# Planner of a three-layer kernel: engine start times, eight warm-up products, and newly chosen order numbers

## Chip, cores and metric

One core of one Trainium2 chip runs the whole program in one launch. The metric is the device time of one execution in microseconds (us). Lower is better.

## The reference

Three layers follow each other on 4 x 576 tokens of width 512, in float32:

```python
q_d, k_d, v_d = means over 4 neighbouring positions       # 144 positions
out = repeat(softmax(q_d k_d^T / 8) v_d, 4) + softmax(mask(|i-j| < 4, q k^T / 8)) v
x = out, heads side by side                                # [4, 576, 512]
xk, xr = mu * x + (1 - mu) * x_prev
x1 = sigmoid(xr @ w_r) * (relu(xk @ w_k) ** 2 @ w_v)       # 512 -> 1024 -> 512
y  = x1 + relu(layer_norm(x1) * g @ w_ch1) @ w_ch2         # 512 -> 2048 -> 512
```

All weights arrive as 64-bit floats and are turned into 32-bit ones on the chip.

## The kernel before

**Work and stages.** The attention runs 16 times, once for each pair of heads of each of the four batches (`attention(n, ...)`, n = 0 to 15). TensorE transposes q and k for some n (`tq`; the others are transposed by VectorE, line 542), and makes the scores of the two heads inside a window (`sc`, line 629, each opened by a mask product on line 623), the scores of the means (`ds`), the transposed weights (`tp`), sums of v (`vs`, the first four n only), and the two outputs (`up`, `pv`). The result lands in `xT`, which holds one batch.

The first dense layer runs over six chunks of 384 tokens. Each takes `prep` (lines 796 to 806: `tmu`, then a high and a low part, `xrh`/`xrl` and `xkh`/`xkl`, for each of four slices of the width), `moe_r` (product `psr`, 36 matmuls of 512 columns), `moe_k` (product `psk`, 96 of 384), `accumulate` (product `psv`, 72 of 512), and `moe_x` (line 861, `r`). A product of float32 accuracy is three matmuls of high and low parts (`mm3`, lines 778 to 780). Chunk 0 needs attentions 0 to 3, chunk 1 needs 0 to 7, and so on, so attentions 4 to 15 lie among the products of chunks 0 to 2. The second dense layer runs three times over 768 tokens (products `psh` and `pso`).

**Weights.** `load_f32` (line 383 on) brings 128 rows of a weight in with one transfer of 512 KB (line 389), into one of two buffers (`w`); ScalarE (lines 395, 397) and VectorE (402, 406) make the 32-bit number of it. `load_split` then makes a high part (line 375 on ScalarE or 376 on VectorE) and a low part (line 420). `wr0l` is the low part of rows 0 to 127 of w_r, `wk31l` that of slice 3, half 1 of w_k.

**What sets the order.** Nothing is issued while the kernel is written down: `add` (line 77) notes each operation with its engine, an estimated cost and a priority. `Plan.order` (line 122) then plays the operations through with these costs, an engine at a time: of what is ready, the one that can start first goes next, with ties decided by priority. It gives each engine its order, and where an operation may run on several engines (`either`, `copy`, `psum_copy`), its engine. The priorities are sums of the numbers in `PRM` (line 24). One of them, `thin`, is a limit in us: when TensorE has done short attention products for longer than it, these rank behind the dense ones. All transfers are issued by SyncE, in the planned order.

`Plan.issue` (line 228) walks through that order. Until the bank of the first `psv` is taken, it fills gaps that the plan shows on TensorE with warm-up products, whose result nobody reads (line 433):

```python
            if eng == "PE":
                if until.t is None:
                    for _ in range(int((o.at - free) / fill_cost)):
                        fill()
                free = o.at + cost
```

The planned gap divided by 0.14 us is the number of fillers. Besides these, 17 warm-up products are issued first of all (`warm_up`, line 431), and two ahead of each score of the first four attentions.

## Time and profile before

| | us |
|---|---|
| median of 3 runs | 773.99 |
| lowest and highest | 770.59, 775.18 |
| the profiled execution | 771.95 |
| its span, first to last instruction | 770.2 |
| TensorE busy in the span | 753.6 |
| VectorE, ScalarE, GpSimd busy | 524.6, 398.2, 63.8 |

The profile is of one execution. PE is TensorE's matmuls, PEld its weight loads, DVE is VectorE, ACT ScalarE, POOL GpSimd, and SP SyncE, whose queue (SPq) issues the transfers. Busy time is a share of the span; a matmul that waits inside its row is drawn busy. An arrow `[1.02 <-ACT ups]` behind a row is the engine's idle time before it and what ended it.

### The profile page before, as it was taken

The numbers are of one execution on the slowest core, as the hardware profiler recorded it, in microseconds if no ns is written. First come the engines' busy times: TensorE is split into PE (matmuls) and PEld (weight loads), VectorE is DVE, ScalarE is ACT, GpSimd is POOL, SyncE is SP. The second block draws the span as 40 slices with busy tenths as digits, with TensorE's granted clock in tenths as the row PEclk, the third lists the DMA queues.
The fourth block names the chain that finished last, engine by engine and source line by source line (L and its number), as shares of the span: only waits on it lengthen the run. The fifth ranks groups of instructions, "written<-read, shape, count | busy, mean of one in ns | idle before, by whom it ended". The sixth has DMA issues, their size and how long they took to land.

```text
span 770.2 us, 15665 instructions
## 1 busy us (share of the span) xinstructions
PE 753.6 (98%) x5816; PEld 650.2 (84%) x5816; DVE 524.6 (68%) x1083; ACT 398.2 (52%) x916; POOL 63.8 (8%) x113
## 2 busy tenths in 40 slices
PE   9999999999999999999999999999999999999997
PEld 6878787788788798888888888889889899889886
DVE  6899999998985959878889763486543364333233
ACT  6889997987884847868835431221421131111110
POOL 3101122112100000000110000020000020000000
PEclk9999999999999999999999999999999999999999
DMA  8997596867768895964689894379853347443322
GB/s 190 208 192 180 180 180 124 182 170 144 207 159 267 251 323 171 290 217 135 141 281 289 208 258 121 112 246 305 183 150 115 112 121 258 138 120 113 123 69 82
DMA packets 202854, 140.88 MB, mean 183 GB/s; under 512 B 127120, under 2 KB 160028, under 8 KB 202780
## 3 DMA queue, kind: packets, MB, share of 16 engines
q1 hardware_dynamic: 202780, 139.90, 66.6%
q8 instruction: 46, 0.75, 0.4%
q14 instruction: 28, 0.23, 0.1%
HBM read 107.88 MB, written 31.98 MB: 182 GB/s over the span
## 4 chain that ended last, share of the span: by engine, by line
PE 77%; DVE 10%; DMA 6%; ACT 4%; issue 2%; POOL 0%; SPq 0%; DVEq 0%; POOLq 0%; ACTq 0%
PE pso L779 8%; PE pso L778 8%; PE pso L780 8%; PE psh L778 7%; PE psh L779 7%; PE psh L780 7%; PE psk L778 4%; PE psv L778 4%; PE psk L780 3%; PE psk L779 3%; PE psv L779 3%; PE psv L780 3%; DMA w<-in_moe_w_ch_dram 3%; PE warm L433 2%; DVE tmu L802 1%
## 5 line engine op out<-in xcount | busy, mean ns | idle before, releaser
L778 PE MATMUL psh<-xn,sa 128*128 128x384 f32 x336 | 114.0, 339 | 2.4 <-DVE c L1114 1.2
L779 PE MATMUL psh<-xn,sa 128*128 128x384 f32 x336 | 113.6, 338 | 0.0
L780 PE MATMUL psh<-xn,sa 128*128 128x384 f32 x336 | 113.3, 337 | 0.0
L778 PEld LDWEIGHTS psh<-xn,sa 128*128 128x128 f32 x336 | 63.1, 188 | 11.0 <-DVE c L1114 2.1
L779 PEld LDWEIGHTS psh<-xn,sa 128*128 128x128 f32 x336 | 63.1, 188 | 6.1 <-DVE xn L1051 0.2
L780 PEld LDWEIGHTS psh<-xn,sa 128*128 128x128 f32 x336 | 63.1, 188 | 0.0
L379 ACT ACTIVATE c22h<-t 128x384 fp32r<-128x384 f32 x24 | 12.6, 525 | 83.7 <-DVE t L1106 78.6
L395 ACT ACTIVATE wf<-w 128x512 f32<-128x512 f32 x48 | 32.3, 673 | 17.4 <-DMA w<-in_moe_w_ch_dram 9.2
L402 DVE SCALAR_TENSOR_TENSOR wf<-wf,w 128x512 uint32<-128x512 uint32 x48 | 32.9, 687 | 11.1 <-ACT w L397 10.6
L379 ACT ACTIVATE kr<-psk 128x384 f32<-128x384 f32 x46 | 22.4, 488 | 25.2 <-PE psk L780 21.2
L379 ACT ACTIVATE c11h<-psh 128x384 fp32r<-128x384 f32 x23 | 11.3, 491 | 45.8 <-PE psh L780 45.7
L397 ACT ACTIVATE w<-w 128x512 uint32<-128x512 uint8 x52 | 35.0, 672 | 0.0
L843 DVE TENSOR_TENSOR kl<-kr,kh 128x384 fp32r<-128x384 f32 x43 | 23.8, 553 | 14.6 <-ACT kr L842 14.3
L1083 DVE SCALAR_TENSOR_TENSOR c11l<-psh,c11h 128x384 fp32r<-128x384 f32 x24 | 13.3, 554 | 29.1 <-ACT c11h L379 29.1
L802 DVE SCALAR_TENSOR_TENSOR tmu<-xT,oms,tmu 128x384 f32<-128x384 f32 (+1 forms) x64 | 31.7, 512 | 1.8 <-ACT tmu L796 1.8
L406 DVE SCALAR_TENSOR_TENSOR wf<-w,wf 128x512 uint32<-128x512 uint32 x48 | 32.7, 680 | 0.3
L1106 DVE TENSOR_TENSOR t<-psh,t 128x384 f32<-128x384 f32 x24 | 13.3, 554 | 28.5 <-PE psh L780 28.4
L1097 DVE TENSOR_TENSOR u<-psh,u 128x384 f32<-128x384 f32 x24 | 13.3, 555 | 27.2 <-PE psh L780 27.1
L379 ACT ACTIVATE c12h<-c 128x384 fp32r<-128x384 f32 x24 | 12.6, 525 | 37.0 <-DVE c L1110 36.9
L379 ACT ACTIVATE c21h<-c 128x384 fp32r<-128x384 f32 x24 | 12.6, 523 | 34.6 <-DVE c L1114 34.6
L796 ACT ACTIVATE tmu<-xT,vecs 128x384 f32<-128x384 f32 (+1 forms) x51 | 26.8, 539 | 6.9 <-DVE xrl L806 4.0
L1103 DVE TENSOR_TENSOR t<-psh,u 128x384 f32<-128x384 f32 x24 | 13.2, 552 | 20.2 <-PE psh L780 20.1
(527 smaller groups left out, 2164.5 us busy)
## 6 DMA issues: line engine op xcount, KB each, us to landing
sa<-s_dram SPq DMA_DIRECT2D x168, 256.0 KB, 2.7
w<-in_moe_w_ch_dram SPq DMA_DIRECT2D x32, 512.0 KB, 6.2
s_dram<-s SPq DMA_DIRECT2D x56, 256.0 KB, 4.0
vw<-in_v_dram SPq DMA_DIRECT2D x62, 96.0 KB, 4.0
x_dram<-r SPq DMA_DIRECT2D x18, 256.0 KB, 3.4
x1t<-x_dram SPq DMA_DIRECT2D x6, 768.0 KB
z_dram<-x1t SPq DMA_DIRECT2D x18, 256.0 KB, 2.7
zb<-z_dram SPq DMA_DIRECT2D x96, 48.0 KB, 2.8
```

The source lines that it names most:

```text
L379: return [("ACT", c_act(n, True), lambda: nc.scalar.activation(dst(), src(), AF.Relu), False), ("DVE", c_dve(n), lambda: nc.vector.tensor_ ...
L395: add("ACT", c_act(512), prio, lambda: nc.scalar.activation(f(), w64().bitcast(F32)[:, :, 1], AF.Abs, scale=2.0 ** -112), r=[w64], w=[f])
L397: add("ACT", c_act(512), prio, lambda: nc.scalar.activation(w64()[:, :, 0], w64().bitcast(U8).rearrange("p a (b c) -> p a b c", c=4)[:, :, ...
L402: lambda: nc.vector.scalar_tensor_tensor(fu(), fu(), 3, w64()[:, :, 0], op0=ALU.logical_shift_left, op1=ALU.bitwise_or),
L406: lambda: nc.vector.scalar_tensor_tensor(fu(), w64()[:, :, 1], 0x80000000, fu(), op0=ALU.bitwise_and, op1=ALU.bitwise_or),
L433: nc.tensor.matmul(warm()[:, :304], identb, isumb, start=True, stop=True)
L778: nc.tensor.matmul(ps, lh, rh, start=start, stop=False, skip_group_check=more)
L779: nc.tensor.matmul(ps, lh, rl, start=False, stop=False, skip_group_check=more)
L780: nc.tensor.matmul(ps, ll, rh, start=False, stop=stop, skip_group_check=more)
L796: add([("ACT", c_act(n, ap=1), lambda t=t, o=o, n=n, cur=cur, kt=kt: nc.scalar.mul(t()[:, o:o + n], cur(), mu[:, kt:kt + 1]), False), ("DV ...
L802: lambda t=t, o=o, n=n, prv=prv, kt=kt: nc.vector.scalar_tensor_tensor(t()[:, o:o + n], prv(), om[:, kt:kt + 1], t()[:, o:o + n], op0=ALU. ...
L843: add(either(C, lambda e: e.tensor_tensor(kl(), kr(), kh().bitcast(F32), op=ALU.subtract)), 0, prio, None, r=[kr, kh], w=[kl])
```

## The change

The planner lets each engine begin at a time of its own instead of at 0, and starts its count of fillers there; the first warm-ups are 8 instead of 17, with a planned cost of 1.55 us instead of 4.5; the loads of q and k of attention 0 are planned with a latency of 1.4 instead of 2.2 us; one small VectorE operation is planned with 0.35 instead of 0.18 us. All numbers of `PRM` that set priorities are new ones, chosen with a judge outside the kernel that halves TensorE's clock behind sparse stretches. Lines behind the second insertion stand five lower in the changed kernel (861 becomes 866), those before it two (389 becomes 391).

```diff
 PRM = dict(
-    thin=89.915, t0=-16.294, t1=-9.875, t2=6.158, t3=7.667, t4=48.796, t5=19.99, t6=6.382, t7=-23.592, t8=-0.47,
+    thin=2.825, t0=-27.784, t1=-16.919, t2=11.055, t3=15.08, t4=55.388, t5=22.947, t6=11.802, t7=-10.22, t8=4.811,
...
+    START = {"PE": 1.78, "ACT": 2.0, "DVE": 2.6, "POOL": 6.6, "SP": 0.74, "CTL": 0.0}
...
-        free = {e: 0.0 for o in ops for e, *_ in o.ways}
+        free = {e: self.START[e] for o in ops for e, *_ in o.ways}
...
-        free = 0.0
+        free = self.START["PE"]
...
-    def warm_up(n=17):
+    def warm_up(n=8):
...
+        LAT = 1.4 if n == 0 else 2.2
...
-                ), w=[dst], lat=2.2)
+                ), w=[dst], lat=LAT)
...
-        add("DVE", 0.18, pr(0.5), lambda: nc.vector.tensor_scalar_add(stat()[:, 0:15], stat()[:, 0:15], 1e-9),
+        add("DVE", 0.35, pr(0.5), lambda: nc.vector.tensor_scalar_add(stat()[:, 0:15], stat()[:, 0:15], 1e-9),
...
-    add("PE", 4.5, -20.0, warm_up, w=[warm])
+    add("PE", 1.55, -20.0, warm_up, w=[warm])
```

In the program as it is issued, the warm-ups and fillers number 162 instead of 135; 35 instead of 24 of them stand ahead of the first `tq`, and 155 instead of 128 ahead of the first `psr`.

**SyncE, the loads up to the last one of w_r.** `kin`, `qin`, `vw` and `v` are the attention's inputs, `w_...` a weight's buffer. Before:

```order
22 L389 DMA w_522<-in_moe_w_k_dram 128x1024
23 L515 DMA vw<-in_v_dram 32x12x64 x4
24 L484 DMA kin<-in_k_dram 96x6x64 x2
25 L389 DMA w_630<-in_moe_w_k_dram 128x1024
26 L484 DMA qin<-in_q_dram 96x6x64 x2
27 L515 DMA vw<-in_v_dram 32x12x64 x4
28 L492 DMA kin<-in_k_dram 32x18x32 x4
29 L389 DMA w_832<-in_moe_w_k_dram 128x1024
30 L492 DMA qin<-in_q_dram 32x18x32 x4
31 L389 DMA w_954<-in_moe_w_r_dram 128x1024
```

Now:

```order
21 L391 DMA w_520<-in_moe_w_r_dram 128x1024
22 L520 DMA vw<-in_v_dram 32x12x64 x4
23 L391 DMA w_589<-in_moe_w_k_dram 128x1024
24 L489 DMA kin<-in_k_dram 96x6x64 x2
25 L489 DMA qin<-in_q_dram 96x6x64 x2
26 L520 DMA vw<-in_v_dram 32x12x64 x4
27 L391 DMA w_783<-in_moe_w_k_dram 128x1024
28 L497 DMA kin<-in_k_dram 32x18x32 x4
29 L497 DMA qin<-in_q_dram 32x18x32 x4
30 L391 DMA w_903<-in_moe_w_k_dram 128x1024
31 L391 DMA w_997<-in_moe_w_r_dram 128x1024
```

The third load of w_r has moved behind attention 2's q and k, and eight loads of weights instead of seven stand ahead of the fourth.

**TensorE, between the first two attentions.** These are the last filler, and the transposes (`tp`), v sums (`vs`) and outputs (`pv`, `up`) of attention 1. Before, with 16 fillers in a row that end with row 200, behind a score of attention 2 that has eight ahead of it:

```order
200 L433 MATMUL warm<-isum,identb 128x304
201 L707 MATMUL tp<-isum,pd 72x2x64 x6
202 L604 MATMUL vs<-vw,wsum 72x128 x6
203 L748 MATMUL pv<-PT,vw 64x96 x6
204 L718 MATMUL up<-pdT,vd 64x144 x4
205 L748 MATMUL pv<-PT,vw 64x96 x6
```

Now, with 36 fillers in a row that end with row 235:

```order
235 L435 MATMUL warm<-isum,identb 128x304
236 L628 LDWEIGHTS identb
237 L628 MATMUL sc<-maskb,identb 128x192
238 L634 MATMUL sc<-kT,qT 32x32 x23
239 L634 MATMUL sc<-kT,qT 24x32
240 L712 MATMUL tp<-isum,pd 72x2x64 x3
241 L609 MATMUL vs<-vw,wsum 72x128 x6
242 L712 MATMUL tp<-isum,pd 72x2x64 x3
243 L435 LDWEIGHTS identb
244 L435 MATMUL warm<-isum,identb 128x304
245 L753 MATMUL pv<-PT,vw 64x96 x12
246 L723 MATMUL up<-pdT,vd 64x144 x4
```

Attention 2's first score has moved behind all of these fillers, and attention 1's transposes behind that score.

**TensorE, around the first psr.** `sc` are the two heads' scores of attention 4. Before:

```order
325 L623 MATMUL sc<-maskb,identb 128x192
326 L629 MATMUL sc<-kT,qT 32x32 x23
327 L629 MATMUL sc<-kT,qT 24x32
328 L623 LDWEIGHTS identb
329 L623 MATMUL sc<-maskb,identb 128x192
330 L629 MATMUL sc<-kT,qT 32x32 x23
331 L629 MATMUL sc<-kT,qT 24x32
332 L778 MATMUL psr<-wr0h,xrh 128x512
333 L779 MATMUL psr<-wr0l,xrh 128x512
```

Now, from the eighth group of three of psr on:

```order
411 L783 MATMUL psr<-wr3h,xrh 128x512
412 L784 MATMUL psr<-wr3l,xrh 128x512
413 L785 MATMUL psr<-wr3h,xrl 128x512
414 L628 LDWEIGHTS identb
415 L628 MATMUL sc<-maskb,identb 128x192
416 L634 MATMUL sc<-kT,qT 32x32 x23
417 L634 MATMUL sc<-kT,qT 24x32
418 L783 MATMUL psr<-wr0h,xrh 128x512
```

The first of the two scores has moved between the eighth and the ninth group of psr, the other one behind the first nine products of psk.

**VectorE, the end of chunk 0.** `r` is chunk 0's closing product of each third of its tokens, `psv` the bank that it frees. Before, the second and the third:

```order
259 L861 TENSOR_TENSOR r<-psv_1501,r 128x512
260 L640 TENSOR_REDUCE mx<-sc 128x6
261 L542 STREAM_TRANSPOSE kT<-kin 128x576
262 L643 TENSOR_TENSOR e<-sc,mx 128x192
263 L542 STREAM_TRANSPOSE qT<-qin 128x576
264 L806 TENSOR_TENSOR xkl<-tmu,xkh 128x384
265 L677 TENSOR_REDUCE stat<-e 128x12
266 L802 SCALAR_TENSOR_TENSOR tmu<-xT_164,oms,tmu 128x192
267 L802 SCALAR_TENSOR_TENSOR tmu<-xT_168,oms,tmu 128x192
268 L861 TENSOR_TENSOR r<-psv_1526,r 128x512
```

Now, all three:

```order
229 L866 TENSOR_TENSOR r<-psv_1501,r 128x512
230 L866 TENSOR_TENSOR r<-psv_1510,r 128x512
231 L807 SCALAR_TENSOR_TENSOR tmu<-xT_178,oms,tmu 128x192
232 L767 TENSOR_TENSOR xT_184<-pv,ups 128x288
233 L807 SCALAR_TENSOR_TENSOR tmu<-xT_184,oms,tmu 128x192
234 L767 TENSOR_TENSOR xT_184<-pv,ups 128x288
235 L807 SCALAR_TENSOR_TENSOR tmu<-xT_178,oms,tmu 128x192
236 L807 SCALAR_TENSOR_TENSOR tmu<-xT_184,oms,tmu 128x192
237 L811 TENSOR_TENSOR xrl<-tmu,xrh 128x384
238 L866 TENSOR_TENSOR r<-psv_1522,r 128x512
```

The second and third closing products have moved forward to the first one.

## Rows read from the trace of the kernel before

**Rows 1.** The page: busy us by engine, share of the span, instructions.
```profile
PE 753.6 (98%) x5816; PEld 650.2 (84%) x5816; DVE 524.6 (68%) x1083; ACT 398.2 (52%) x916; POOL 63.8 (8%) x113
```

**Rows 2.** Windows by stage: length, busy us (instructions) by engine, granted clock, DMA share, GB/s.
```profile
0.00:45.61 45.61, 43.10 (x761) 33.23 (x763) 36.02 (x88) 34.17 (x96) 8.27 (x36) 1.00 0.99 192
45.61:57.31 11.70, 10.11 (x205) 8.17 (x205) 10.45 (x22) 8.76 (x22) 1.30 (x2) 1.00 1.03 213
57.31:72.00 14.69, 14.59 (x85) 11.94 (x78) 14.69 (x29) 13.81 (x29) 3.53 (x4) 1.00 0.82 171
72.00:200.00 128.00, 125.49 (x1719) 102.85 (x1719) 119.28 (x262) 109.43 (x295) 26.77 (x50) 1.00 0.71 162
200.00:381.00 181.00, 177.45 (x1174) 152.71 (x1173) 144.95 (x300) 133.12 (x282) 6.81 (x7) 1.00 0.77 224
381.00:768.00 387.00, 382.82 (x1888) 341.28 (x1886) 199.17 (x387) 98.95 (x198) 17.12 (x14) 1.00 0.56 170
```

**Rows 3.** Timeline of SyncE's queue: start, length; the third and fourth load of w_r.
```profile
19.92 0.43 SPq L389 DMA_DIRECT2D w<-in_moe_w_r_dram  x1
...
45.61 1.71 SPq L389 DMA_DIRECT2D w<-in_moe_w_r_dram  x1
```

**Rows 4.** Chain of work that ended last: start, length, what; 45 to 58 us.
```profile
45.61 6.70 DMA w<-in_moe_w_r_dram
...
53.16 0.59 ACT w L397
...
57.01 0.84 DVE wr0l L420
```

**Rows 5.** Timeline of TensorE, opening: start, length, matmul, shape, count, idle before.
```profile
1.78 4.69 PE L433 MATMUL warm<-isum,identb 128*128 128x304 bf16 x24 [1.78 <-DVE identb L326]
...
6.40 1.21 PE L555 MATMUL tq<-isum,kin 96*64 96x96 f32 x24
...
25.77 2.24 PE L433 MATMUL warm<-isum,identb 128*128 128x304 bf16 x16
...
27.85 0.82 PE L707 MATMUL tp<-isum,pd 128*72 128x128 f32 x6
...
53.21 0.38 PE L561 MATMUL tq<-isum,kin 96*128 96x96 f32 x2 [1.02 <-ACT ups L371]
...
55.86 0.24 PE L623 MATMUL sc<-maskb,identb 128*128 128x192 bf16 x1
...
57.31 0.49 PE L778 MATMUL psr<-wr0h,xrh 128*128 128x512 f32 x1
57.90 0.50 PE L779 MATMUL psr<-wr0l,xrh 128*128 128x512 f32 x1
```

**Rows 6.** Timelines of TensorE, then of VectorE, around 71 us.
```profile
70.23 0.82 PE L433 MATMUL warm<-isum,identb 128*128 128x304 bf16 x5
70.79 0.44 PE L778 MATMUL psk<-xkh,wk30h 128*128 128x384 f32 x1
71.07 0.39 PE L779 MATMUL psk<-xkl,wk30h 128*128 128x384 f32 x1
...
72.00 0.43 PE L433 MATMUL warm<-isum,identb 128*128 128x304 bf16 x2
72.27 0.25 PE L623 MATMUL sc<-maskb,identb 128*128 128x192 bf16 x1
```

```profile
70.41 0.55 DVE L806 TENSOR_TENSOR xkl<-tmu,xkh 128x384 fp32r<-128x384 f32 x1
```

**Rows 7.** VectorE's groups by shape: busy us, mean ns of one, idle before.
```profile
L402 DVE SCALAR_TENSOR_TENSOR wf<-wf,w 128x512 uint32<-128x512 uint32 x48 | 32.9, 687 | 11.1 <-ACT w L397 10.6
...
L585 DVE TENSOR_REDUCE qd<-qT 128x144 f32<-128x576 f32 x10 | 7.4, 740 | 0.0
...
L591 DVE TENSOR_TENSOR v<-v 72x512 f32<-72x512 f32 x10 | 7.3, 726 | 0.3 <-DMA v<-in_v_dram 0.3
```

**Rows 8.** Timeline of TensorE: the first product of the second layer.
```profile
380.44 0.34 PE L778 MATMUL psh<-xn,sa 128*128 128x384 f32 x1
```

More of the change, by code (lines that the diff above doesn't have):

```diff
@@ L24 @@
 PRM = dict(
-    thin=89.915, t0=-16.294, t1=-9.875, t2=6.158, t3=7.667, t4=48.796, t5=19.99, t6=6.382, t7=-23.592, t8=-0.47,
-    t9=-5.238, t10=-2.702, t11=0.12, t12=5.747, t13=-8.176, t14=-15.681, t15=-4.758, m0=2, m1=1, m2=0, m3=3, m4=1,
+    thin=2.825, t0=-27.784, t1=-16.919, t2=11.055, t3=15.08, t4=55.388, t5=22.947, t6=11.802, t7=-10.22, t8=4.811,
+    t9=-1.564, t10=-2.876, t11=1.822, t12=2.572, t13=-9.18, t14=-3.928, t15=-14.768, m0=2, m1=1, m2=0, m3=3, m4=1,
     m5=0, m6=0, m7=2, m8=3, m9=0, m10=0, m11=0, m12=0, m13=0, m14=0, m15=0, g0=0, g1=0, g2=0, g3=0, g4=0, g5=0, g6=0,
@@ L28 @@
     g7=0, g8=0, g9=0, g10=0, g11=0, g12=0, g13=0, g14=0, g15=0, h0=1, h1=1, h2=1, h3=1, h4=0, h5=0, h6=0, h7=0, h8=0,
-    h9=0, h10=0, h11=0, h12=0, h13=0, h14=0, h15=0, dve=0.27, pool=0, ta=-14.632, u0=4.274, tl=26.492, tm=4222.228,
-    ld=33.163, ldv=76.41, mu=-14.605, wr=-0.059, wrs=-31.134, wka=-33.615, wkas=7.94, wkb=12.502, wkbs=-165.286,
-    wv=103.601, wvs=2.875, wld=0.932, d0=235.165, d1=108.349, d2=260.708, d3=463.399, d4=581.694, d5=82886.056,
-    a1=13.725, a1s=43.62, a1l=52.7, a2=-1.632, a2s=26.831, a2l=56.61, a3=54.215, a3s=40.382, a3l=96.628, xr=-60.685,
@@ L33 @@
-    xrs=16.307, xk=22.171, xks=1.12, xrn=9, xrns=1.512, xkn=-4.695, xkns=17.37, w2a=10.707, w2as=1.55, w2=7.281,
-    w2s=34.846, wc=10.079, wcs=106.739, m2q=8, sld=-6.173, x1=3, wcg=-39.001, p0l=11.872, p0=2.352, p0s=3.263,
-    p0n=7.723, dp=684.729, ra0=-8.097, ra1=-1.757, ra2=3.642, ra3=4.616, ra4=-5.44, ra5=0, rb0=0.342, rb1=19.209,
-    rb2=16.653, rb3=33.463, rb4=10.116, rb5=0, rx0=-2.918, rx1=-13.421, rx2=8.601, rx3=12.062, rx4=-2.926, rx5=5.409,
-    ne=12, we=52.842, wes=25.704, wel=6.378,
+    h9=0, h10=0, h11=0, h12=0, h13=0, h14=0, h15=0, dve=0.281, pool=0, ta=-6.788, u0=0.998, tl=28.334, tm=1512.554,
@@ new lines @@
+    ld=-14.61, ldv=692.556, mu=-16.27, wr=2.694, wrs=-40.653, wka=-1.496, wkas=-16.907, wkb=3.303, wkbs=-551.681,
+    wv=86.573, wvs=2.803, wld=3.024, d0=234.157, d1=108.178, d2=245.252, d3=203.157, d4=407.252, d5=573537.1,
+    a1=12.275, a1s=43.588, a1l=50.967, a2=-3.593, a2s=26.051, a2l=57.611, a3=50.028, a3s=41.284, a3l=104.853,
+    xr=-5.985, xrs=4.399, xk=7.333, xks=19.976, xrn=9, xrns=0.307, xkn=-9.411, xkns=16.533, w2a=11.654, w2as=1.571,
+    w2=7.98, w2s=53.045, wc=-0.309, wcs=66.56, m2q=8, sld=-6.79, x1=3, wcg=-6.595, p0l=5.189, p0=1.25, p0s=4.959,
@@ L38 @@
+    p0n=12.645, dp=891.68, ra0=-4.514, ra1=-16.19, ra2=-14.341, ra3=0.246, ra4=-10.084, ra5=0, rb0=-3.67, rb1=15.946,
+    rb2=-11.455, rb3=7.107, rb4=6.113, rb5=0, rx0=2.169, rx1=51.31, rx2=-2.07, rx3=-6.387, rx4=8.037, rx5=13.405,
+    ne=12, we=60.989, wes=21.242, wel=1.221,
 )
@@ L486, in load @@
                         in_=src[b, 2 * u + hp].rearrange("(c p) d -> p c d", c=6),
-                    ), w=[(dst, hp)], lat=2.2)
+                    ), w=[(dst, hp)], lat=LAT)
                 return
@@ L494, in load @@
                         in_=src[b, 2 * u + hp, :, 32 * e:32 * e + 32].rearrange("(c i) d -> i c d", i=32),
-                    ), w=[(dst, (hp, e))], lat=2.2)
+                    ), w=[(dst, (hp, e))], lat=LAT)
         load(k, kin)
```

## The prediction

> **What bounds the kernel now.** I read the stages first, because a share over the whole span hides them [rows 1, 2]. TensorE is drawn busy 753.6 of 770.2 us, its granted clock is 1.00 in every stage, and of the last stage's 387 us it has 382.8 full: there nothing but fewer products could help. The opening is different. Up to 57.31 us, where the first product of the gate projection (psr) starts, TensorE does four attentions and 128 warm-ups; in the first 45.61 us the 16 DMA engines stand at a share of 0.99, while VectorE has 36.0 of 45.6 us. So the opening is paced by transfers and by the chains behind them, and warm-ups only fill what TensorE would wait. From 57.31 to 72 us VectorE is full (14.69 of 14.69); from 72 to 200 us TensorE has 125.5 and VectorE 119.3 of 128 us: two engines that take turns in setting the end.
>
> Then the queue and the chain. Of the four loads of w_r, two stand at the head of SyncE's queue and two at 19.92 and 45.61 us [rows 3]. The last one is a step of the chain that ended last: 6.70 us for the transfer, then ScalarE, then VectorE's wr0l, which ends at 57.85 [rows 4]; psr's second product starts at 57.90 [rows 5].
>
> **The change, part by part.** The steps START, LAT, the two costs and the eight warm-ups alter nothing that the chip does by themselves: they are numbers with which the planner sets the order and the count of fillers. What reaches the chip is an order and 162 warm-ups in place of 135. The total work of ScalarE, VectorE and GpSimd is the same but for a few instructions that change their engine.
>
> *The tail.* TensorE's order is the same, row for row, from behind the last product of the last attention (about 235 us) to the end, VectorE's too but for neighbours that change places. So the last 530 us cost 0 more or less, and whatever happens before is carried to the end one for one.
>
> *The opening.* Eight warm-ups are not eight: the fillers add 27 at once, and 35 stand ahead of the first transpose (tq) where 24 did. Up to the first psr there are 155 for 128. A warm-up at full pace takes 2.08/16 = 0.130 us (25.77 to 27.85, [rows 5]), so 27 more are 3.5 us. The two scores of attention 4 have moved behind the start of psr; they began at 55.86 and ended at 57.31, which takes 1.45 us out [rows 5]. If TensorE's queue sets the moment: +2.1 us. If the fillers only take what was idle or waited: below zero, down to -1.45. Transfers: wr0's load now has 59 transfers and 9381 KB ahead of it for 58 and 8869 KB (counted in SyncE's order); one load of a weight, 512 KB, is more by 2.7 us at the 192 GB/s of that stretch [rows 2]. VectorE: ahead of wr0l stand three more instructions of a weight (0.69 us each), and out of the way went two sums of v (0.73 and a shorter one), a sum of q (0.74) and a few small ones [rows 7]: 0 within 1 us. These three are not added, since the latest of them decides; the ends are -1.45 and 2.1 + 2.7 = +4.8. I take **+1.5**, nearer to TensorE's and VectorE's own than to the transfer's, because the chain of rows 4 has ScalarE and VectorE work to do while wr0 is awaited.
>
> *From the first psr to 72 us.* TensorE now does the two scores here (+1.45) and no longer the five and two warm-ups at 70.23 and 72.00 (70.79 - 70.23 = 0.56, and 0.27 up to the next score at 72.27; [rows 6]). The five stood in a wait: the product at 71.07 needs xkl's fourth piece, which VectorE ends at 70.96 [rows 6]. VectorE has 134 instructions ahead of that piece before and after. So the scores are partly hidden there: between 0 (all hidden) and +0.65 (1.45 - 0.83); I take **+0.5**.
>
> *72 to 235 us.* The order of both engines is shuffled by a few places. Two of chunk 0's three closing products (r, line 861) stand about 13 us of VectorE's work earlier, chunk 1's xkl pieces about 4.7 us earlier, one xrl later; two v sums, two weight remainders and three remainders of xr differ in engine, so that VectorE has 1.8 us less up to the common tail (each instruction ahead of it at the mean of its group). TensorE changes from short attention products to long ones 48 times for 46. The bounds: VectorE's idle of 8.7 us of the 128 [rows 2] is what at most could go, and half as much could come anew: -8.7 to +4.4. I take **-1.5**, nearest to the 1.8 us that VectorE loses in work.
>
> **The sum.** +1.5 + 0.5 - 1.5 = +0.5 us on the profiled execution, which took 771.95 us (770.2 of span and 1.75 around it): 772.5. The median of the runs shown, 773.99, is 2.0 above that execution, so in its terms 774.5. I write 773, between the two. A measurement of this kernel can tell about 1% (7.7 us) from no change, and the sum is far inside that.
>
> **The rivals.**
> *Fillers in the way (slower).* Place: behind attention 0's last product. Eight warm-ups stood there before attention 2's score and 16 more before attention 1's transposes (tp); now 36 stand in one piece, 4.7 us, and tp comes behind them and the score. If the operands are there as early as before, tp moves from 27.85 by 12 x 0.130 + 0.72 = 2.3 us, the first tq by 11 x 0.130 = 1.4 us, and the last load of w_r adds its 2.7: the first psr at 57.31 + 6.4, then +0.5 and no gain after it, so 779 and with one turn of VectorE's queue more (another 2) 781. For it: in rows 5 tp starts in the very moment in which the 16 end, so the queue, not the operand, may have held it. Against it: the DMA share of 0.99, which says that the operands of attentions 2 and 3 come late by themselves. It decides if the first psr starts after 62.5 us.
> *Stalls that go (faster).* Place: 72 to 200 us. If the earlier closing products free the accumulators, and VectorE runs through, most of its 8.7 us of idle and the 1.8 less of work come off the end, with an opening that stays where it was: 771.95 - 8.5 + 0.5, or 764. For it: what the order moved forward is just what frees accumulators. Against it: TensorE is idle for only 2.5 of those 128 us, and it has two more changes of kind.
> [...]
>
> **Chances.** The forecast (little moves) 0.70; fillers in the way 0.12; stalls that go 0.16; the clock 0.02. The first lies within 1% by itself, the second and the fourth are slower, the third faster by over 1%, which gives 0.16, 0.70 and 0.14. The range reaches from just below the faster rival to just above the slower one, 763 to 782, and leaves out what is beyond either. The likeliest case's own range, from its terms' ends taken by half, is 768 to 778.
>
> **What would show it.** Right: the first psr between 57 and 61 us; psk's fourth step (wk30) at 71 to 73; the second layer's products (psh) starting within 3 us of the 380.44 of before [rows 8], and behind that start an unchanged stretch of 770.2 - 380.4 = 389.8 us; a granted clock of 1.00 throughout. Wrong: a first psr before 55 or after 62.5, a stage from 72 to 235 us that is shorter or longer by more than 4 us, or a slice in which the clock is below 1.00.

## The result and the profile after

The changed kernel takes 779.07 us (median of 15 runs, 773.72 to 784.82), the kernel before in the same comparison 770.93 (15 runs, 769.26 to 775.18): a ratio of 1.0102, with a 95% interval of 1.0081 to 1.0122. The change costs 8 us. The forecast was 773.0 and "within 1%", from a sum of +0.5 us for the change; the time lies inside the range of 763 to 782, but the sum missed a loss of 8 us. The profiled execution took 779.14 us, 777.4 of it span, for 771.95 and 770.2 before.

The page of the changed kernel answers to [rows 1] and adds the queues (packets, MB, share of 16 engines) and the warm-ups' group:

```profile
PE 758.7 (98%) x5843; PEld 654.4 (84%) x5843; DVE 525.6 (68%) x1079; ACT 397.1 (51%) x918; POOL 66.7 (9%) x116
...
q8 instruction: 46, 0.75, 0.4%
...
L435 PE MATMUL warm<-isum,identb 128*128 128x304 bf16 x162 | 27.2, 314 | 3.2 <-DVE identb L328 1.8
```

TensorE is drawn busy 5.1 us longer for 27 products more. The stages, with the bounds of [rows 2]:

```profile
0.00:45.61 45.61, 42.18 (x744) 31.83 (x745) 33.20 (x78) 28.55 (x78) 8.72 (x37) 1.00 1.01 202
45.61:57.31 11.70, 11.28 (x122) 9.30 (x121) 11.40 (x28) 11.16 (x31) 0.00 (x0) 1.00 0.45 125
57.31:72.00 14.69, 13.36 (x130) 10.79 (x127) 13.40 (x27) 11.84 (x25) 4.40 (x3) 1.00 0.59 168
72.00:200.00 128.00, 127.41 (x1783) 104.75 (x1782) 121.54 (x262) 112.04 (x302) 29.54 (x55) 1.00 0.78 165
200.00:381.00 181.00, 174.74 (x1154) 150.20 (x1152) 139.31 (x289) 128.52 (x275) 5.25 (x6) 0.99 0.75 220
```

From 72 to 200 us TensorE now waits only 0.6 of 128 us (2.5 before). The stage behind it has 6.3 us without a product (3.6 before) and a granted clock of 0.99.

Following the same product through both timelines shows where the 8 us came from (us after minus before):

```
first psr            57.31 ->  60.94   +3.63
first psk            65.97 ->  71.09   +5.12
chunk 1, first psr  126.99 -> 130.57   +3.58
chunk 1, first psk  143.10 -> 142.28   -0.82
chunk 2, first psk  210.34 -> 211.15   +0.81
chunk 2, 37th psk   227.46 -> 234.56   +7.10
first psh           380.44 -> 387.51   +7.07
```

The opening loses 3.6 us and the first stage of psr another 1.5; by 211 us all but 0.8 is won back; then 23.4 us lose 6.29, and that is carried to the end. The last two stretches do not hold the same work, though. The kernel before does these 18 products of an attention ahead of chunk 2's first psk (TensorE's timeline):

```profile
208.85 0.95 PE L655 MATMUL ds<-kd,qd 64*64 64x144 f32 x12
209.73 0.85 PE L707 MATMUL tp<-isum,pd 128*72 128x128 f32 x6
210.34 0.42 PE L778 MATMUL psk<-xkh,wk00h 128*128 128x384 f32 x1
```

In the changed kernel 12 `ds` and 6 `tp` more stand behind that psk, 1.5 us of work. On equal work 2.8 us are won back by 211 us, not 4.3, and 4.8 are lost behind it. The changed kernel's timeline of TensorE there (start, length, matmul, count, idle before):

```profile
220.20 0.62 PE L634 MATMUL sc<-kT,qT 64*32 64x32 f32 x48
220.75 0.45 PE L783 MATMUL psk<-xkh,wk20h 128*128 128x384 f32 x1
...
221.21 0.33 PE L785 MATMUL psk<-xkh,wk20l 128*128 128x384 f32 x1
224.22 0.33 PE L783 MATMUL psk<-xkh,wk30h 128*128 128x384 f32 x1 [2.67 <-issue]
...
224.82 1.23 PE L660 MATMUL ds<-kd,qd 64*64 64x144 f32 x12
225.98 1.49 PE L712 MATMUL tp<-isum,pd 128*72 128x128 f32 x6
227.13 0.67 PE L783 MATMUL psk<-xkh,wk00h 128*128 128x384 f32 x1
227.59 0.52 PE L784 MATMUL psk<-xkl,wk00h 128*128 128x384 f32 x1
227.91 0.52 PE L785 MATMUL psk<-xkh,wk00l 128*128 128x384 f32 x1
```

and the same stretch as windows (columns as in [rows 2]):

```profile
211.15:221.21 10.06, 9.30 (x178) 7.39 (x169) 8.56 (x23) 8.32 (x23) 0.15 (x1) 1.00 1.15 254
221.21:224.22 3.01, 0.34 (x3) 0.19 (x3) 1.70 (x5) 0.61 (x2) 0.00 (x0) 1.00 0.80 112
224.22:226.00 1.78, 1.78 (x16) 1.15 (x15) 0.00 (x0) 1.02 (x3) 0.00 (x0) 0.82 0.08 15
226.00:228.00 2.00, 2.00 (x11) 1.83 (x10) 1.74 (x4) 1.83 (x6) 0.00 (x0) 0.50 0.00 0
228.00:230.00 2.00, 2.00 (x11) 1.91 (x9) 1.03 (x3) 1.00 (x6) 0.00 (x0) 0.81 0.14 53
230.00:234.56 4.56, 4.56 (x50) 3.81 (x48) 3.56 (x9) 4.17 (x10) 0.00 (x0) 1.00 0.45 149
```

TensorE stands still for 2.67 us with "issue" as the releaser: no engine and no data transfer that the profile names was being waited for, and the product behind the standstill carries no wait for a semaphore in the trace. Behind the standstill the granted clock falls to 0.50 (window from 226 to 228 us), and products of 384 columns that start every 0.17 us elsewhere start every 0.32. Between 224.22 and 230.00 us the clock's mean is 0.71, which is 5.78 x 0.29 = 1.7 us lost. Of the 6.29 us, standstill and clock make 4.4, the moved products 1.5, and a wait for a load of vw at 216.6 makes 0.59; small waits on both sides are the rest.

What does TensorE wait for? The transfers in a window at the standstill (queue: packets, MB, share of 16 engines):

```profile
DMA packets 693, 0.21 MB, mean 159 GB/s; under 512 B 686, under 2 KB 686, under 8 KB 692
...
q1 hardware_dynamic: 692, 0.19, 107.4%
q8 instruction: 1, 0.02, 5.7%
```

This is 221.5 to 222.8 us. The instruction queue q8 moves one piece of 16 KB in it, which starts at 221.54, when TensorE runs dry, and takes 1.18 us; TensorE goes on 1.5 us after its end. There are 46 such pieces in the span, and TensorE's recorded instructions (5843 products, 5843 weight loads, 271 steps of its sequencer) are 11957, about 256 for each. When TensorE ran dry it had begun 6337 of them, which is 24 x 256 + 193. That remainder tells what the wait is for. The 20 traces of this study hold 28 waits of 0.2 us or more that end with "issue"; 27 of them lie behind a multiple of 256 plus exactly 193 instructions (449, 705, 1217, 1473 or 6337), and in all 27 TensorE goes on 1.3 to 1.7 us after the end of one piece's transfer. Counting the instructions between the starts of pieces gives 256, 289 and 219 behind 262 us, where long products run, but 466 between 195.24 and 213.56 us, 313 from there to 221.54, and 32 to the next at 225.93. So TensorE's program comes in pieces of 256 instructions, and two in a row came late in a stretch in which the short products of the attentions use them up fast.

The opening has a smaller case of the same, at 449 instructions (columns as in [rows 5]):

```profile
1.78 7.19 PE L435 MATMUL warm<-isum,identb 128*128 128x304 bf16 x35 [1.78 <-DVE identb L328]
...
8.90 1.21 PE L560 MATMUL tq<-isum,kin 96*64 96x96 f32 x24
...
18.40 1.60 PE L435 MATMUL warm<-isum,identb 128*128 128x304 bf16 x11 [1.38 <-issue]
...
27.17 4.82 PE L435 MATMUL warm<-isum,identb 128*128 128x304 bf16 x36
...
32.55 0.52 PE L712 MATMUL tp<-isum,pd 128*72 128x128 f32 x3
...
60.94 0.49 PE L783 MATMUL psr<-wr0h,xrh 128*128 128x512 f32 x1
```

The first 35 warm-ups start 0.253 us apart up to 6.83 us and 0.129 apart behind.

The chain of work that ended last (start, length, what) runs through this wait and through fillers, and no longer through the last load of w_r as in [rows 4]:

```profile
17.02 1.38 issue
...
27.24 4.76 PE warm L435 x36
...
45.04 3.08 PE warm L435 x23
```

### The profile page after: what moved, and what is told of

It is laid out like the page before. It is cut to its first block, busy times and chain, and to the rows that moved or that the text cites. A ratio compares the mean times of both kernels' runs of the same rounds, so it can differ in the third digit from the quotient of the medians.

```text
span 777.4 us, 15717 instructions
## 1 busy us (share of the span) xinstructions
PE 758.7 (98%) x5843; PEld 654.4 (84%) x5843; DVE 525.6 (68%) x1079; ACT 397.1 (51%) x918; POOL 66.7 (9%) x116
## 4 chain that ended last, share of the span: by engine, by line
PE 76%; DVE 9%; DMA 5%; ACT 5%; issue 3%; POOL 1%; SPq 0%; DVEq 0%; POOLq 0%; ACTq 0%
PE pso L784 8%; PE pso L783 8%; PE pso L785 8%; PE psh L783 7%; PE psh L784 7%; PE psh L785 7%; PE psk L783 3%; PE warm L435 3%; PE psk L785 3%; PE psk L784 3%; PE psv L783 3%; PE psv L784 3%; PE psv L785 3%; PE pv L753 2%; PE sc L634 2%
## 5 line engine op out<-in xcount | busy, mean ns | idle before, releaser
L435 PE MATMUL warm<-isum,identb 128*128 128x304 bf16 x162 | 27.2, 314 | 3.2 <-DVE identb L328 1.8
```

The costliest lines, as they stand in the source:

```text
L435: nc.tensor.matmul(warm()[:, :304], identb, isumb, start=True, stop=True)
```

## The experiments

The theories: **A**, the late program pieces, above all the one near 222 us, carry the loss. **B**, the opening's fillers do. **C** and **D**, the new table's order of 72 to 235 us costs it by itself, through waits for data and other engines, and pieces are a detail. Two more on what makes a piece late: **E**, only the pace of short products; **F**, small packets ahead of it. A gap filler is a warm-up that the planner puts into a gap (130 of the 162).

All runs in one table: median; its ratio to the kernel before in the same comparison, with the 95% interval; then, of the profiled execution, the first psr, the stretch from the first to the 37th psk product of chunk 2, and the issue waits of 0.2 us or more. The runs below the first two have 4 to 12 executions each, and the last three columns are of one of them: for old_table (788.04 us) and old_opening (777.00) it lies well above the median.

```
                    us      ratio, 95% interval        psr    stretch  issue waits (at)
before            770.93                              57.31   17.12   0.24 (41)
after             779.07  1.0102 (1.0081 to 1.0122)   60.94   23.41   1.38 (18), 2.67 (224)
fill_narrow       780.21  1.0128 (1.0091 to 1.0165)   64.55   22.07   0.25 (11), 0.75 (16), 3.23 (47), 1.97 (229)
fill_halfsplit    775.86  1.0071 (1.0043 to 1.0100)   63.92   18.80   0.59 (20)
old_table         782.27  1.0141 (1.0105 to 1.0178)   58.79   17.27   2.39 (44)
new_table         785.13  1.0186 (1.0152 to 1.0220)   67.23   19.06   2.47 (20), 1.39 (49)
fill_split27      776.85  1.0092 (1.0063 to 1.0121)   60.12   21.78   1.54 (221)
fill_split86      776.50  1.0079 (1.0056 to 1.0102)   64.19   18.20   1.36 (22)
before_halfsplit  772.30  1.0023 (1.0006 to 1.0041)   57.24   16.63   0.77 (20)
convert_late4     784.88  1.0186 (1.0161 to 1.0210)   62.70   17.87   2.01 (18)
wide_after        775.07  1.0066 (1.0039 to 1.0094)   62.91   18.18   none
wide_before       772.52  1.0031 (1.0007 to 1.0056)   59.34   17.06   none
first24           778.27  1.0119 (1.0079 to 1.0159)   61.80   20.21   2.57 (18), 1.71 (225)
first24_s130      775.23  1.0058 (1.0026 to 1.0090)   64.01   19.04   2.21 (21)
old_opening       773.06  1.0038 (1.0014 to 1.0062)   58.55   19.04   0.38 (43)
old_opening_split 777.53  1.0079 (1.0047 to 1.0112)   58.67   22.76   0.22 (15), 0.91 (36), 0.82 (41)
new_opening       785.28  1.0171 (1.0138 to 1.0203)   64.88   18.25   1.93 (19), 0.73 (48), 0.65 (235)
before_traffic6   772.39  0.9999 (0.9977 to 1.0020)   56.84   17.14   1.20 (42)
before_traffic12  772.13  1.0009 (0.9995 to 1.0022)   57.60   17.50   0.93 (43)
before_small12    777.44  1.0080 (1.0050 to 1.0109)   57.02   22.72   0.65 (42)
```

**Where the pieces lie.** A filler is two instructions of TensorE, so cutting fillers in two moves the borders of the 16 KB pieces against the work and leaves the fillers' time as it is (two products of 152 columns take 0.13 us, as one of 304 does).

```diff
-    plan.issue(lambda: warm_up(1), 0.14, pvs[0][2])
+    plan.issue(filler, 0.14, pvs[0][2])
+    def filler():
+        n_fill[0] += 1
+        k = 1 + n_fill[0] % 2
+        for _ in range(k):
+            nc.tensor.matmul(warm()[:, :304 // k], identb, isumb[:, :304 // k], start=True, stop=True)
```

That is fill_halfsplit; fill_narrow has one product of 152 columns each time, and fill_split27 and fill_split86 have `k = 2 if n_fill[0] <= 27` (or 86) `else 1`.

> The changed kernel, each of its 130 gap fillers with 152 columns instead of 304 (their products are used by nothing); order and number of TensorE instructions stay as in the changed kernel. Theory A (the late program piece: TensorE's instructions come in pieces of 16 KB, the piece that it needs at 222 us lands late, 2.7 us of standstill and a half clock behind it; the opening's +3.6 us is won back by 211 us anyway): the standstill near 222 us stays, 778 us, within 2 us of the changed kernel. Theory B (the fillers of the opening stand in the way and the end carries it): the first product of psr comes 3 us earlier and so does the end, 775 us. Theory C (the new table's order of the stretch 72 to 235 us costs it, with no regard to pieces): 778 us, but with the loss spread over the stretch rather than in one standstill.

> The changed kernel, every second gap filler cut into two of 152 columns: same columns, same order, 65 products more, so TensorE's program is 130 instructions longer ahead of everything that follows and the borders of its 16 KB pieces lie half a piece earlier in the work. Theory A: the standstill at 222 us moves or goes; 772 to 775 us if it goes, and up to 783 if it falls worse. Theory B and theory C: no difference, 779 us within 1.5.

> The changed kernel, its first 27 gap fillers (those ahead of the first tq, where the clock is low) each cut into two of 152 columns: TensorE's program is 54 instructions longer ahead of all that follows. Theory A (late program pieces): the opening as in the changed kernel (first psr near 61 us), the standstill at 222 us moves or changes its length; 774 to 776 us without it, 777 to 783 with it. Theory D (the new order of the stretch 72 to 235 us, and the waits for data in it, cost the time, and pieces only fill a wait that would be there anyway): 779 us within 1.

> As the run with 27, but 86 gap fillers are cut in two: 172 instructions more, two thirds of a piece. Theory A: the standstill near 222 us is gone or elsewhere, as with 130 instructions more; 774 to 777 us, if the opening stays within 1 us of the changed kernel's. Theory D: 779 us within 1.

With the pieces in place (fill_narrow) the standstill returns at the same product; with 130 or 172 instructions more it is gone from there, and the stretch falls from 23.41 to 18.80 and 18.20 us. With 54 more it sits a few products earlier:

```profile
220.57 0.55 PE L642 MATMUL sc<-kT,qT 64*32 64x32 f32 x24 [1.54 <-issue]
```

and this one too has a half clock behind it (0.50 from 220.57 to 222 us, 0.52 from there to 224); it lies again behind 6337 instructions. Three shifts take 2.2 to 3.2 us off the median. That speaks for A and against D, which had 779 us for the last two, though of A's numbers (772 to 775 for fill_halfsplit, 777 to 783 for fill_split27 with a standstill left, 774 to 777 for fill_split86) only the last was met.

The shifts move more than pieces. In fill_halfsplit and fill_split86, and in first24_s130 and wide_after below, ScalarE's pdT is waited for near 57 us for 1.85 to 3.26 us, the mean granted clock of the profiled execution is 0.995, 0.998, 0.996 and 0.997, and chunk 2 starts 1.4 to 4.8 us later than in the changed kernel. In fill_halfsplit the twelve pv products behind the wait take 1.23 us, in wide_after 0.72. What the median shows is the gain of the stretch less this loss. In fill_split86 almost nothing is left of it (its 37th psk is 0.37 us earlier): 2.5 of the 2.9 us that its profiled execution gains come behind the first psh, where TensorE idles 0.8 us for 3.0. Of all these only fill_split27 leaves the opening nearly as it was (first psr at 60.12).

Theory B's 775 for fill_narrow did not come: thinner fillers brought psr later, not earlier, with an issue wait of 3.23 us in the opening, behind which twelve ds products take 1.71 us (0.95 in the kernel before at 208.85), and a mean granted clock of 0.993 in the profiled execution.

**Fillers out, pieces kept.** first24 leaves 11 fillers out ahead of the first tq and cuts 11 others in two, so that the count of instructions stays; first24_s130 cuts 76.

```diff
+        i = n_fill[0]
+        k = 0 if i <= 11 else 2 if i <= 22 else 1
```

> The changed kernel with 24 filler times ahead of the first tq, as before had, instead of 35: 11 fillers left out and 11 others cut in two, so TensorE's program is as long as in the changed kernel and its pieces lie the same. Theory A: first tq about 2 us earlier, the end within 1.5 us of the changed kernel, for the standstill at 222 us stays. Theory B (fillers in the way): first psr and the end both 2.5 us earlier, 776.5 us.

> As first24, with 76 fillers cut in two, so TensorE's program is 130 instructions longer than in the changed kernel. Theory A: no issue wait near 222 us and the half clock behind it gone, 773 to 775.5 us. Theory B: as first24, 776.5 us.

First24's timeline of TensorE:

```profile
17.90 1.79 PE L444 MATMUL warm<-isum,identb 128*128 128x304 bf16 x9 [2.57 <-issue]
...
225.00 0.34 PE L792 MATMUL psk<-xkh,wk30h 128*128 128x384 f32 x1 [1.71 <-issue]
```

The first tq starts at 7.21 us for 8.90, and the piece at 15.1 us is then waited for 2.57 us instead of 1.38: most of the 1.7 us is given back at once, and behind that wait the granted clock is 0.50 from 19 to 22 us, where the changed kernel has 1.00. The late pieces of 213.6 and 221.5 us come again, at 215.1 and 222.5, and stop the same product. With 130 instructions more that wait is gone and the median is 3.0 us lower. B's 2.5 us did not come: without the 11 fillers the median is 0.8 us lower, and the ratio is not lower at all. But this is no clean test of B, since the longer wait and the half clock came in the fillers' place; what the fillers cost in the changed kernel is not shown by it.

**Fewer, wider fillers.** 74 of 512 columns in place of 130 of 304 (54 in wide_before).

```diff
-    plan.issue(lambda: warm_up(1), 0.14, pvs[0][2])
+    plan.issue(filler, 0.235, pvs[0][2])
+    def filler():
+        nc.tensor.matmul(warm()[:, :].rearrange("p (a n) -> p a n", a=2), identb,
+                         isumb[:, :256].rearrange("p (a n) -> p a n", a=1).to_broadcast([P, 2, 256]),
+                         start=True, stop=True)
```

> The changed kernel, gap fillers of 512 columns instead of 304 and as many fewer (71 instead of 130): the same filler time, TensorE's program 118 instructions shorter in the opening. Theory A (late program pieces): fewer instructions are wanted in the opening, so the issue wait of 1.4 us before 18.4 us goes and the first psr comes 1.5 to 2.5 us earlier; the standstill near 222 us moves; 774 to 777 us. Theory D (order and data waits alone): 779 us within 1.

> The kernel before with the same wide fillers. Theory A: before has only one short issue wait (0.24 us), so there is little to gain: 769 to 772 us, with first psr within 1 us of 57.3. Theory D: the same, 771 us within 1.

No issue wait is left in either. But the first psr of wide_after comes at 62.91 us, 2 us later than in the changed kernel, where A had it 1.5 to 2.5 earlier. ScalarE's timeline and then TensorE's say why:

```profile
55.82 0.66 ACT L397 ACTIVATE wf<-w 128x512 f32<-128x512 f32 x1 [1.42 <-DMA w<-in_moe_w_r_dram]
```

```profile
56.82 0.72 PE L758 MATMUL pv<-PT,vw 128*64 128x96 f32 x12 [3.26 <-ACT pdT L721]
```

In its planned order ScalarE stands before the last load of w_r, an attention's step (pdT) stands behind that, and TensorE behind the step. In this run TensorE is not late by its pieces, and waits for the weight: one wait takes the place of the other (3.26 us here for 1.38 in the changed kernel). wide_before, also without an issue wait, is no faster than the kernel before: there were 0.24 us to gain, and its psr comes 2 us later behind waits of 0.3 to 1.1 us for ScalarE; its 772.52 lies half a us above what both theories had. The changed kernel is not of this kind: its last load of w_r is issued at 50.25 us, when VectorE has freed the buffer, lands at 53.77, and ScalarE takes it up at 54.62 without having idled for it.

**The parts alone.** old_table is the changed planner (START, LAT, the sum's cost, 8 warm-ups) with the table of before; new_table is the reverse. Their diffs are the parts of the diff above.

> The planner part of the change alone (begin of each engine, load latency, sum's cost, 8 warm-ups at 1.55) with the table of before. Theory A: near the kernel before, 771 us, unless a piece falls late. Theory B: the opening has about as many fillers as the changed kernel, so 774 to 775 us. Theory C: 771 us, since the order of the stretch 72 to 235 us is set by the old table.

> The table of the change alone, with the planner of before (17 warm-ups, engines free at zero). Theory A: depends on where a piece falls late; 771 us without a standstill behind 200 us, 777 us with one. Theory B: 771 to 775 us. Theory C: 778 us, as the table sets the order of the stretch.

Each part alone is slower than the two together: 782.27 and 785.13 us. No theory had that. The due times and the planner's clock fit each other, and the effects of the parts do not add up; "which part costs the 8 us" has no answer in this form. In old_table psr waits 3.44 us for ScalarE at 69.3, and its first product behind that takes 0.80 us (0.49 in the changed kernel at 60.94, at a clock of 1.00); in new_table two pieces are late, and the clock is 0.50 from 21 to 27 us, behind the first.

**Old and new order, cut at the first psr.** The planner runs with its own due times until it reaches the first psr, and then takes those of the other table, in the same list of operations.

```diff
+            if not switched and found[eng][0] >= SWITCH:
+                switched = True
+                prio[:] = LATER
+                rank()
+                for t in parked:
+                    ready += parked[t]
+                    parked[t] = []
+                continue
```

`LATER` holds the due times of the other kernel, `SWITCH` is 56.4 (old_opening) or 60.0 (new_opening) on the planner's clock, and `rank()` sorts the buffers again that are not yet taken. old_opening_split has fillers cut as in fill_halfsplit.

> The kernel before up to the first psr (its planner numbers, its table, order word for word the same), and from there the due times of the changed table. Theory A: the new table's order behind the opening costs nothing by itself and even gains (in the changed kernel 2.8 us are won back between 61 and 211 us), so without a late piece 768 to 771 us; with one near 215 to 225 us (an issue wait over 1 us there) 772 to 776. Theory D (the new order of 72 to 235 us costs the time): 775 to 778 us with no issue wait to show for it.

> As old_opening, every second gap filler cut into two of 152 columns, so that the pieces of TensorE's program lie elsewhere. Theory A: a different time from old_opening wherever one of the two has an issue wait over 1 us and the other none, by 2 to 4 us; else the same within 1.5 us. Theory D: the same within 1 us.

> The changed kernel up to the first psr, and from there the due times of the old table. If the opening alone costs (fillers, issue waits and the late loads of w_r, which bring psr 3 to 5 us later): 774 to 776 us. Theory A with the opening won back: 771 to 773 us, unless a piece lands late behind 190 us. Theory D: 771 us within 1.5, since the old order of 72 to 235 us is back.

The new order behind the old opening costs 2.9 us (a ratio of 1.0038); A had 768 to 771 us and D 775 to 778, and 773.06 meets neither. The waits of the profiled execution are for ScalarE, not for pieces:

```profile
114.65 0.72 PE L1017 MATMUL pv<-PT,vw 128*64 128x96 f32 x12 [1.76 <-ACT ups L640]
...
219.64 0.72 PE L1017 MATMUL pv<-PT,vw 128*64 128x96 f32 x12 [1.46 <-ACT ups L640]
```

So much of D holds: the new order brings waits that no piece causes. Yet the 12 executions run from 770.04 to 779.92 us, and the five whose granted clock is 0.999 or more have a median of 771.88: more than half of the 2.9 us goes with the clock's fall in the others. In old_opening_split no piece is late behind 50 us, but products of the attention wait for ScalarE again, 2.01 us at 180 and 2.17 at 222. Behind the first, products of 512 columns start every 0.43 us (every 0.23 at a clock of 1.00), and behind the second the clock falls, as the windows from 220 us on show:

```profile
220.00:224.00 4.00, 2.23 (x65) 1.69 (x65) 2.81 (x7) 3.00 (x11) 0.15 (x1) 0.98 0.66 205
224.00:226.00 2.00, 2.00 (x53) 1.88 (x53) 2.00 (x7) 1.43 (x4) 0.00 (x0) 0.50 0.77 183
226.00:230.00 4.00, 4.00 (x22) 3.09 (x21) 2.09 (x6) 2.83 (x8) 0.00 (x0) 0.50 0.58 185
```

The clock's fall is thus not a matter of pieces: it comes behind these waits for ScalarE (0.57 from 115 to 117 us in old_opening, 0.50 from 224 to 230 in old_opening_split) as behind the standstill. A's "no issue wait, no difference" and D's "the same" fell here. new_opening at 785.28 misses every theory: the old due times behind the new opening are worse than both pure kernels.

**The kernel before, shifted.**

> The kernel before, every second gap filler cut into two of 152 columns (about 85 instructions more ahead of psr). Theory A: the kernel before has a piece that lands 3 us late at 224 us without a standstill, so a shift can make one there or in the opening: 771 to 777 us, and where it is slower by over 2 us the trace shows an issue wait of over 1 us on TensorE. Theory D: 771 us within 1, as order and columns are unchanged.

The fillers are cut as in fill_halfsplit. The profiled execution has the same span within 1 us (769.4), an issue wait of 0.77 us that is made good by 143 us, and no standstill behind that; the ratio is 1.0023, under a quarter of the change's. This one shift brings the kernel before no late piece behind the opening.

**What makes a piece late.** convert_late4 moves the loop of early conversions behind the last attention in the list and makes the loads of the last 8 depend on it:

```diff
+            done = len(plan.ops) - 1
...
+                n0 = len(plan.ops)
                 w1_convert(*w1_parts(g, j)[i % 4][1:], start[1] + PRM["we"] + PRM["wes"] * i)
+                if i >= EARLY:
+                    plan.ops[n0].deps.add(done)
```

> The changed kernel, with the loads of the last 8 of 12 early conversions of w_ch1 held until the last attention is done (they lay between about 195 and 232 us). Takes 4 MB of loads and stores and the conversions' VectorE and ScalarE work out of the stretch in which the piece lands late. Theory A: pieces land in time, no issue wait over 1 us behind 190 us, clock 1.00 there; 773 to 775 us. Theory D: the stretch gains too, but by fewer waits on VectorE and ScalarE and not by the issue wait; 776 to 778 us. Both lose if the conversions are then late for psh: over 780 us.

As A had it, no issue wait is left behind 190 us, and the stretch is free of any wait, at full clock:

```profile
212.73:230.60 17.87, 17.87 (x258) 15.15 (x250) 13.09 (x34) 13.51 (x43) 0.15 (x1) 1.00 0.37 101
```

But the conversions come in the way later (psr waits 2.73 us for ScalarE's xrh at 354, and up to 360 us its products behind that take 0.63 us and more, for 0.39), and it loses 6 us to the changed kernel, as both theories had it for this case. Since its order changed with its transfers, three more runs add transfers alone to the kernel before: behind the loads of w_ch1, or behind those of vw, into memory that nothing reads (the edit of before_small12):

```diff
                 nc.sync.dma_start(out=dst[:, g0:g1, :], in_=src)
+                if n >= 13:
+                    nc.sync.dma_start(out=spare[n - 13, j, :, g0:g1, :], in_=src)
```

> The kernel before with six transfers of 256 KB added to SyncE's queue behind the loads of w_ch1 between about 195 and 230 us (from w_ch1 to a place in memory that nothing reads); the order and number of instructions on all other engines is unchanged. Theory A (TensorE's program pieces wait behind data transfers): the pieces at 207 to 234 us come later than before and an issue wait of over 1 us appears on TensorE between 205 and 235 us, with 2 to 6 us more at the end. Theory E (pieces come late only because short products use them up fast, whatever the transfers do): no issue wait over 0.5 us there; what is lost is waits named DMA, 0 to 2 us.

> As before_traffic6, with all twelve early loads of w_ch1 doubled so (from about 110 us on). Theory A: issue waits of over 0.5 us also between 110 and 195 us where short products stand close, 3 to 8 us in all. Theory E: none.

> The kernel before with each of the twelve loads of vw of the last three attentions (202 to 218 us, 96 KB in elements of 256 bytes) issued a second time, into memory that nothing reads; the order and number of instructions on all other engines is unchanged. Theory F (small packets ahead of it make TensorE's program piece late): an issue wait of over 1 us on TensorE between 205 and 230 us, or pieces there that start 4 us later than before; 773 to 778 us. Theory E (short products alone): no issue wait over 0.5 us there; waits named DMA vw of 0.5 to 3 us may come, 771 to 774 us.

The added transfers of 256 KB change nothing: six or twelve of them leave the time (ratios 0.9999 and 1.0009) and the stretch (17.14 and 17.50 us for 17.12) as they were, and move the pieces of 206.7, 216.3 and 223.7 us by at most 1.1 us (six) and 2.0 (twelve). The small packets cost 6 us (777.44 for 770.89 in the same comparison), but not through pieces: these three start up to 1.7 us earlier than before. What comes late is data:

```profile
213.49 0.69 DVE L595 TENSOR_TENSOR v<-v 72x512 f32<-72x512 f32 x1 [3.07 <-DMA v<-in_v_dram]
```

```profile
215.15 0.66 ACT L395 ACTIVATE wf<-w 128x512 f32<-128x512 f32 x1 [3.31 <-DMA w<-in_moe_w_ch_dram]
```

These are VectorE's and ScalarE's timelines in before_small12; TensorE's tp then waits for ScalarE's pd four times, 3.8 us in all. So theory F fell as it was put, and E held for the issue waits, though its 771 to 774 us did not. But the added transfers hardly tested E: the DMA share from 205 to 215 us was 1.16 before and is 1.00 with six of them. The 20 traces taken together speak against pace alone. In calm stretches a piece starts when TensorE is some 25 instructions short of the border ahead of the one where it is needed. Measured from there, the 536 pieces up to 270 us start in the median at once where the DMA share of the ten us before was below 0.5, 2.0 us late where it was 0.7 to 0.9, and 3.7 us late above 1.1; the piece of 221.54 us in the changed kernel is 6.5 us late at a share of 1.14. That is a connection and not a test. Why exactly the pieces of 213.6 and 221.5 us are late stays open.

No version in the study beats the kernel before.

## Why the prediction was wrong, step by step

- **The tail, 0.** Right: +7.07 us at the first psh stand for +7.10 at 234.56, and from psh to the end of the span it is 389.85 us for the 389.8 named, in the same order of products. That the length fits so well is partly luck: over the 20 traces it lies between 387.3 and 391.3 us, by waits of TensorE for VectorE and ScalarE that come and go.
- **The opening, +1.5 (bounds -1.45 to +4.8).** Measured +3.63: inside the bounds, under-sized. The prediction had +2.1 if TensorE's queue sets the moment, and it does: TensorE idles 4.28 us up to the first psr for 4.11 before, the wait for the piece included, so 3.46 of the 3.63 us are its own work. What the term mis-sized are the warm-ups ahead of the first tq: 11 more take 2.50 us (8.90 for 6.40) and not 1.4, since the first 35 run at 0.203 us each. The other end, a later load of w_r, did not count: the load is issued 4.6 us later, but nothing in the changed kernel waits for it. Taking fillers out did not give the time back (first24, fill_narrow), because later pieces (waits of 2.57 us in first24, 3.23 in fill_narrow) and a half clock (0.50 from 19 to 22 us in first24) came instead; so the 3.63 us are read from this one trace, and no run isolates them.
- **The first psr to 72 us, +0.5.** Too small (and its upper end, 1.45 - 0.83, is 0.62 and not 0.65): the first psk is 1.5 us later still, with a wait of 0.90 us for ScalarE's r that the prediction had not named, and wk30's step comes at 75.11 instead of 71 to 73.
- **72 to 235 us, -1.5 (bounds -8.7 to +4.4).** Measured +2.0 from the first psk to 234.56: the step that failed most, by 3.5 of the sum's 6.6. Up to 211 us it was right and even too shy: 2.8 us are won back on equal work. Then 4.8 are lost in 23 us, and of those 4.4 are a late program piece and the half clock behind it. The term was priced by work and by VectorE's idle; a wait that no engine causes had no place in it, although the kernel before shows one of 0.24 us before 41.35.
- **The rivals.** "Fillers in the way" has the nearest times (779 to 781) by a path that is half right: tp came 4.7 us later (32.55 for 27.85; the rival had 3.7 with the first tq), but the first psr at 60.94, short of the 62.5 from which it decides, and most of that was won back by 211 us. "Stalls that go" half happened (0.6 us of TensorE's idle left of 2.5 between 72 and 200 us) and was eaten up. "The clock" (0.02): a half clock did come, from 225.36 to 228.78 us, behind the standstill, and took 1.7 us. It was 0.50 behind 2.67 us of idle here, and behind 2.17 us in old_opening_split. A short wait did not bring it every time: 1.71 us in first24 and 2.31 in convert_late4 (at 272 us) left the clock at 1.00, 1.54 in fill_split27 and 1.76 in old_opening did not. Nor is the 1.00 of the first window of [rows 2] a reading of the start: the trace's clock records begin 4.7 us into the span before and 6.9 us into the one after. That the clock is low ahead of the first tq, as is said for fill_split27, is an estimate from the 0.253 us at which warm-ups start there, for 0.129 behind.
- **The signs.** Of the three that would make it wrong one was met: windows at a clock below 1.00. The first psr (60.94) and the stage from 72 to 235 us (+2.0) stayed inside theirs, because a gain and a loss in that stage nearly cancel; a bound on each half would have caught it. Of the signs of being right the first psr and the 389.8 us came, and wk30 (75.11), psh (+7.07) and the clock did not.

How the 8 us divide: the three kernels with the pieces where the change put them (after, fill_narrow, first24) have ratios of 1.0102, 1.0128 and 1.0119, the five with the pieces elsewhere 1.0071, 1.0092, 1.0079, 1.0066 and 1.0058. The means, 1.0116 and 1.0073, differ by 0.43%, or 3.3 us. Single intervals overlap; that all five lie below all three carries it, though the grouping was made afterwards, one of the five (fill_split27) still has a late piece there, and four bring waits of their own in the opening. The new order behind the old opening is 2.9 us, and the opening would be what is left, some 2. This last is only a difference: the parts do not add up cleanly, as old_table, new_table and new_opening show. The clock runs across these parts. Each execution's mean granted clock is on record: 0.991 to 0.999 in the changed kernel, on average 0.996, and on average 0.999 in 94 executions of the kernel before. By an estimate, 0.004 x 777 = 3.1 us for 0.8, the clock takes 2.3 of the 8 us. In first24_s130 the four executions at 1.00 take 771.21 to 772.93 us, close to the kernel before, and the other six 774.04 to 779.63.

## What to carry to other kernels

Ask of every reordering not only which engine waits for which, but how many instructions an engine has to be fed in a stretch: where hundreds of short products stand close, TensorE can run out of program (here for 2.67 us, where it began 466 and 313 instructions between the starts of pieces), and a change of a few dozen instructions far ahead moves that place (54 in fill_split27). Read "issue" in the list of waits beside the instruction queue's transfers, and count the instructions ahead of it: 27 of the 28 waits here had the same remainder of 256, which is 193. Cutting a filler in two moves the pieces, but, as the shifts show, other waits with them. And price a wait of two us in a thin stretch at more than its length, since the clock may fall behind it, whatever the wait was for: here 2.67 us were followed by 1.7 lost, and 2.17 us in old_opening_split by six us at 0.50. Look at the granted clock of every execution, and not only of the profiled one.

## What was not expected of the hardware

- TensorE's program arrives in 46 pieces of 16 KB, and a late one stops TensorE for 0.2 to 3.2 us, in 27 of 28 cases at the same remainder of 256 instructions, 193. In wide_after and wide_before, with fewer and wider fillers, no such wait is left; in all other kernels but fill_split27 at least one of 0.2 to 3.2 us stands in the opening, where fillers and four attentions are close.
- 1.5 MB and 3 MB more of 256 KB transfers beside the attentions cost nothing that could be measured (ratios 0.9999 and 1.0009); 1.2 MB of 256-byte elements cost 6 us, by data that came 3 us late on VectorE and ScalarE.
- The changed kernel spreads over 11 us in 15 runs, the kernel before over 6. The granted clock differs from run to run and goes with it: the fastest of the 15 (773.72 us) has 0.999, and the three slowest (781.03 to 784.82) have 0.991 to 0.996. How late pieces differ from run to run only profiled executions could show, and there is one for each kernel.
